# Seven-product blocks of an expert layer: when a block's last output matmuls, its input forms and the next block's attention are issued

## The chip, the cores and the metric

The kernel runs on one core of a Trainium2 chip (trn2). The metric is device time in microseconds (us), the median of three runs. The core's engines are named as the profile names them: PE (TensorE matmuls), PEld (its weight loads), DVE (VectorE), ACT (ScalarE), POOL (GpSimd) and SP (SyncE, which issues nearly all DMAs).

## The reference, cut to what matters

Attention over pooled keys and values, then two expert layers, each fed by the one before:

```python
# q, k, v: (8 batches, 8 heads, 576 rows, 64)
k_p = k.reshape(B, H, 72, 8, D).mean(axis=3)      # v_p likewise
attn = softmax(q @ k_p.T / 8) ; x = attn @ v_p    # max subtracted, sum + 1e-9
x = x as (4608, 512)                              # rows by all heads
y = (sigmoid(x @ w_gate) * (x @ w_val)) @ w_out   # d_ff = 1536
h = y @ w_in                                      # d_ff = 2048
out = where(h > 0, h, exp(min(h, 0)) - 1) @ w_out2
```

All inputs and outputs are float32. TensorE gets each float32 operand as a high and a low part, and every product is made in three passes (high·high, high·low, low·high), so that one product of a 128-row operand costs three matmuls.

## The kernel before, in words

The 4608 rows go in nine tiles of 512 rows, n = 0 to 8. Each tile n needs its attention output x (512 features, four feature tiles), then the first expert layer on it, and its y is written to DRAM. The second expert layer (from about 1190 us of the trace on) reads y back. Neither the change nor what follows touches that layer's code.

**Tiles n = 0, 1** run the first layer directly, with 512-column matmuls (the loop up to `SQ` = 2, by twelve chunks c of 128 hidden features). Beside it `plan(m)` lays out the attention of the next tile.

**Tiles n = 2 to 8 ("blocks")** use Strassen's scheme in Winograd's form for x @ w_gate and x @ w_val: x is cut into two halves of rows (`LOW`, `HIGH`, 256 columns) and two halves of features, and from these four quarters `form_x` makes seven forms (a11, a12, a22, s1 to s4), each as a high part (a rounded copy) and a low part (a subtraction). A block has twelve units, u = 0 to 11. An even unit is a chunk pair's gate, the next odd unit its value. Each unit makes seven products in the order `STEPS` (k = 0 to 6), each of six matmuls of 256 columns (line 1166, tiles `pl`). DVE and ACT put the seven products together through `u2`, `u3`, `u4` (lines 1176 to 1208), apply the sigmoid to the gate, and the value unit multiplies the two into `sg` and splits it into the high and low `g`.

**Output matmuls** ("y": line 658, 512 columns, accumulated in four `acc` banks over a whole block) follow the pair of units that made their `g`: 24 a pair, spread over the next two units' steps by `Y_FILL` through the list `fill` (`filler(n)` issues the next n of it).

**Block border.** After unit 11, `weighted` (lines 599 and 606) makes the next block's x from probabilities and values into four PSUM banks, the 24 output matmuls still in `fill` run in one go, `form_x` is written out, and the next block's units 0 and 1 have no output matmuls, since a block's first `g` comes after unit 1. The four finished `acc` banks are copied out at u = 0, k = 1, 2, 3, 6 (`FLUSH_AT`, `flush_one`) and stored.

**Attention of the next block.** `thin_plan(n+1)` hangs steps on (unit, step) positions of block n, each issued behind that step's product and output matmuls. For each of four 128-row tiles i, with u = 2 + 2i: q transposes (`q_thin`, at k = 4), scores in two halves (`s_thin`, at u, 6 and u+1, 1: line 532, with maximum and subtraction on DVE), exponential (`emit_exp`, u+1, 2), sum and normalisation (`emit_norm`, u+1, 3: lines 563 and following) and the transposed probabilities in two halves (`t_thin`, u+2, 0 and 2: line 578). All of these, and the keys' transposes, go through the one PSUM bank `at1`. Sigmoid and exponential stand in different activation tables, so ACT loads a table (`ACT_TABLE_LOAD`) at each change. Keys and values of a batch are loaded in five chunks, pooled on DVE (`pool_k` line 469, `pool_v` line 491) and placed; a block that needs a new batch has its keys loaded and pooled in its predecessor's units 0 to 4, its values in units 3 to 9. Blocks 2 to 6 prepare batches 3 to 7; block 7 has neither keys nor values to prepare.

**Background work.** `work()` takes the next piece of preparing the second layer's weights (loads, narrowing on DVE by lines 107, 111, 117 and 121, stores), 34 pieces a block at the positions `WORK_AT` and `MORE_AT`.

Each engine runs its own instructions in program order (`manual_schedule`): the positions above set the order, and an instruction that waits holds up all behind it on its engine. Output matmuls and products need no DVE step between them except through the product banks (three, `places`, two used twice and one three times a unit) and through `g`.

## Time and profile before

| | |
|---|---|
| median of three runs | 1951.09 us (1948.0 to 1951.66) |
| the profiled execution's own time | 1948.47 us |
| its span in the trace | 1946.8 us |
| PE busy in the span | 1798.2 us (92%) |
| DVE, ACT, POOL busy | 1108.1, 858.1, 635.0 us |
| from a block's `weighted` to the next one's, blocks 2 to 7 | 127.1, 121.8, 120.5, 120.2, 122.6, 112.8 us |

Read a row of the timeline as: start in the span, busy time, engine, line, operation, tile written <- tiles read, partitions x elements, count; in brackets the engine's idle time just before and what ended it. A run of matmuls of one form stands as one row, and its busy time can overlap that of the next row, so for PE the distance between starts is what counts. Rows of waits give a sum, the number of waits and the longest. Rows of windows give the busy time of each engine in a stretch, then the granted PE clock as a share of 2.4 GHz.

### The profile page before, as it was taken

The page shows a single profiled execution, that of the slowest core. Times are in us where ns is not written, and L with a number is a line of the kernel's source. Part 1 is how long each engine was busy: PE and PEld are TensorE (multiplying, and loading weights), DVE is VectorE, ACT ScalarE, POOL GpSimd, SP SyncE. Part 2 cuts the span into 40 slices and gives each one's busy share as a digit, 9 for nine tenths or more (in the row PEclk, how much of TensorE's full clock was granted, in tenths as well). Part 3 has the DMA queues.
Part 4 walks back from the last instruction along what each step waited for, and adds up shares of the span by engine and source line. Part 5 has one row for each costly group of instructions (what it writes and reads, how often), then busy time and mean ns, then how long its engine had stood idle before and what let it go on. Part 6 is the DMA issues. An engine that isn't in the chain of part 4 may idle for free.

```text
span 1946.8 us, 27943 instructions
## 1 busy us (share of the span) xinstructions
PE 1798.2 (92%) x10212; PEld 1587.7 (82%) x10212; DVE 1108.1 (57%) x2073; ACT 858.1 (44%) x1727; POOL 635.0 (33%) x635
## 2 busy tenths in 40 slices
PE   3687899799999999999999899999999999999999
PEld 2465777688887888888889788998998989989987
DVE  6799566666666667666665664533444344443432
ACT  3355344344444444434444334444454444444443
POOL 2345345334243333433333332222222222222222
PEclk8788999899999999999999999999999999999999
DMA  7254344575756757567576887334343353343431
GB/s 204 90 171 156 124 128 146 199 231 192 245 188 228 229 190 248 186 231 237 172 232 207 300 309 281 118 125 168 114 179 116 119 192 127 121 176 132 147 114 52
DMA packets 150905, 346.81 MB, mean 178 GB/s; under 512 B 47728, under 2 KB 79472, under 8 KB 150768
## 3 DMA queue, kind: packets, MB, share of 16 engines
q1 hardware_dynamic: 150768, 345.02, 51.8%
q8 instruction: 81, 1.33, 0.3%
q14 instruction: 56, 0.46, 0.1%
HBM read 287.31 MB, written 57.67 MB: 177 GB/s over the span
## 4 chain that ended last, share of the span: by engine, by line
PE 71%; DVE 18%; ACT 4%; issue 3%; DMA 3%; POOL 1%; SPq 0%; ACTq 0%; DVEq 0%; POOLq 0%
PE oacc L1327 20%; PE bank L1281 18%; PE pl L1166 15%; PE acc L658 9%; DVE nt L117 2%; PE gv L633 2%; PE ats L532 2%; DVE nt L111 1%; DMA rkv<-in_k_dram 1%; DVE nt L107 1%; DVE vs L491 1%; DVE a L95 1%; DVE ks L469 1%; PE pl L599 1%; DVE sm L563 1%
## 5 line engine op out<-in xcount | busy, mean ns | idle before, releaser
L1281 PE MATMUL bank<-form,wr 128*128 128x384 f32 x2016 | 411.0, 338 | 1.0 <-DVE u L1314 0.7
L1281 PEld LDWEIGHTS bank<-form,wr 128*128 128x128 f32 x2016 | 366.5, 188 | 29.1 <-DVE u L1314 1.1
L658 PE MATMUL acc<-g,wos 128*128 128x512 f32 x1152 | 349.5, 399 | 0.9 <-ACT g L94 0.4
L1327 PE MATMUL oacc<-w2o,gc 128*128 128x512 f32 x1080 | 288.9, 393 | 0.4 <-POOL gc L95 0.4
L1327 PEld LDWEIGHTS oacc<-w2o,gc 128*128 128x128 f32 x1080 | 199.6, 187 | 30.5 <-POOL gc L95 0.8
L658 PEld LDWEIGHTS acc<-g,wos 128*128 128x128 f32 x1152 | 192.6, 191 | 15.1 <-ACT g L94 1.2
L95 POOL TENSOR_TENSOR gc<-ea,gc 128x384 fp32r<-128x384 f32 x96 | 98.3, 1024 | 298.2 <-ACT gc L94 295.1
L95 POOL TENSOR_TENSOR g<-sg,g 128x512 fp32r<-128x512 f32 x108 | 142.6, 1330 | 161.7 <-ACT g L94 161.7
L1166 PE MATMUL pl<-s,wg 128*128 128x256 f32 x1008 | 154.7, 290 | 37.7 <-DVE u L1181 27.0
L1166 PEld LDWEIGHTS pl<-s,wg 128*128 128x128 f32 x1008 | 140.8, 192 | 57.6 <-DVE u L1181 37.3
L95 POOL TENSOR_TENSOR gc<-pair,gc 128x384 fp32r<-128x384 f32 x96 | 98.1, 1022 | 260.4 <-ACT gc L94 238.4
L1166 PE MATMUL pl<-s,tt 128*128 128x256 f32 x1008 | 154.9, 291 | 11.5 <-DVE a L95 4.4
L1166 PE MATMUL pl<-a,wg 128*128 128x256 f32 x1008 | 154.1, 289 | 5.0 <-DVE sg L1200 5.0
L1166 PEld LDWEIGHTS pl<-s,tt 128*128 128x128 f32 x1008 | 138.8, 192 | 23.4 <-DVE u L1202 4.7
L633 PE MATMUL gv<-x,wg 128*128 128x512 f32 x576 | 147.6, 411 | 10.0 <-DVE x L95 5.3
L1166 PEld LDWEIGHTS pl<-a,wg 128*128 128x128 f32 x1008 | 140.9, 192 | 18.3 <-DVE sg L1200 9.1
L1327 PE MATMUL oacc<-w2p,gc 128*128 128x512 f32 x540 | 143.2, 393 | 0.0
L633 PEld LDWEIGHTS gv<-x,wg 128*128 128x128 f32 x576 | 111.6, 198 | 36.1 <-issue 7.5
L94 ACT ACTIVATE g<-sg 128x512 fp32r<-128x512 f32 x108 | 68.1, 631 | 153.2 <-DVE sg L1203 102.7
L1327 PEld LDWEIGHTS oacc<-w2p,gc 128*128 128x128 f32 x540 | 99.8, 187 | 14.8
L1198 POOL TENSOR_TENSOR sg<-sg,u 128x256 f32<-128x256 f32 x42 | 33.6, 801 | 206.2 <-DVE u L1197 187.8
L1294 DVE SCALAR_TENSOR_TENSOR ea<-ea,bank 128x384 f32<-128x384 f32 x48 | 26.7, 555 | 117.0 <-ACT ea L1291 117.0
(199 smaller groups left out, 2861.2 us busy)
## 6 DMA issues: line engine op xcount, KB each, us to landing
wr<-wd SPq DMA_DIRECT2D x96, 896.0 KB, 6.4
tt<-td SPq DMA_DIRECT2D x84, 768.0 KB, 5.1
wos<-wd SPq DMA_DIRECT2D x96, 512.0 KB, 5.3
rw<-in_moe_w_out_dram SPq DMA_DIRECT2D x22, 512.0 KB, 3.6
r<-yd SPq DMA_DIRECT2D x24, 384.0 KB, 7.8
out_dram<-po SPq DMA_DIRECT2D x36, 256.0 KB, 2.0
rw<-in_moe_w_in_dram SPq DMA_DIRECT2D x16, 512.0 KB, 4.0
wd<-rw SPq DMA_DIRECT2D x16, 512.0 KB, 5.9
```

Source lines behind the costliest of these rows:

```text
L94: nc.scalar.activation(out=dst_hi, in_=src, func=AF.Copy)
L95: eng.tensor_tensor(out=dst_lo, in0=src, in1=f32(dst_hi), op=ALU.subtract)
L107: nc.vector.tensor_scalar(out=t.bitcast(F32), in0=t.bitcast(F32), scalar1=H_LOW, scalar2=H_HIGH, op0=ALU.max, op1=ALU.min)
L117: nc.vector.scalar_tensor_tensor(out=t, in0=r[:, :, 1], scalar=-0x40000000, in1=t, op0=ALU.bitwise_and, op1=ALU.bitwise_or)
L532: nc.tensor.matmul(a[o:o + n, i // 2, (i % 2) * w:(i % 2 + 1) * w], lhsT=qt[:, j * P + o:j * P + o + n], rhs=kbd[b % 2][:, j * w:(j + 1) * w],
L633: nc.tensor.matmul(d, lhsT=w[:, i, a_w, j], rhs=x[j][:, a_x], start=(j == 0 and a_w == 0 and a_x == 0), stop=(j == KD - 1 and a_w == 1),)
L658: return lambda: nc.tensor.matmul(acc[m], lhsT=w[:, a_w, m * P:(m + 1) * P], rhs=g[:, a_g], start=(c == 0 and a_w == 0 and a_g == 0), stop ...
L1166: nc.tensor.matmul(src, lhsT=w(a_w, j), rhs=f_t[nm][:, j, a_x], start=opens and m == 0, stop=m == 5, skip_group_check=True,)
L1198: nc.gpsimd.tensor_tensor(out=c22, in0=c22, in1=u4, op=ALU.mult)
L1281: nc.tensor.matmul(bank[b ^ flip], lhsT=wp[q][a_w][:, w, j * P:(j + 1) * P], rhs=form_tile(s, a)[j][:, a_x], start=opens and n == 0, stop= ...
L1294: nc.vector.scalar_tensor_tensor(out=e, in0=e, scalar=-1.0, in1=src, op0=ALU.add, op1=ALU.max)
L1327: return lambda: nc.tensor.matmul(acc[t + i], lhsT=g[c][:, a_g, i * P:(i + 1) * P], rhs=wo2[2 * q + e][a_w], start=opens and p == 0, stop= ...
```

## The change

Five things are moved; of the arithmetic, some rounded copies and subtractions in `form_x` go to another engine.

1. **The last output matmuls.** Of the 24 left at the border, seven run before the next block's first product; the others follow by `Y_FIRST` in units 0 and 1. The last twelve go bank by bank (`by_tile`), and `FLUSH_AT` copies the `acc` banks out at (0, 5), (0, 6), (1, 1) and (1, 4).
2. **The forms** come in three portions from a generator: a11, s3 and a12 at the border, s2, s1 and a22 behind step 0 of unit 0, s4 behind step 3. Unit 0 takes its products in the order `FIRST_STEPS`. More of the high parts are made by ACT.
3. **The attention** of a tile stands at u = 1 + 2i: q at k = 0, scores at k = 2 and 4, exponential at k = 5; sum, normalisation and transposes in the unit behind it, at k = 0, 1, 4 and 6. `emit_sum` is a step of its own, ahead of `emit_norm`.
4. **Keys** are loaded and pooled one block earlier: `thin_plan(m)` handles the values of batch m in units 2 to 9 and the keys of batch m + 1 in units 7 to 10. Batch 3's keys are handled at the end of tile n = 1 (`plan`, chunks 8 to 11).
5. **Background work** has other positions, 35 a block, none in unit 0.

The first block (n = 2) issues nine output matmuls and then all three portions at once.

```diff
+    PASSES_Y = ((0, 0), (1, 0), (0, 1))
+    def emit_sum(t, p):
+        sm = at_p.tile([P, H], F32, name="sm", tag="sm", bufs=2)
+        nc.vector.tensor_reduce(out=sm, in_=p.rearrange("p (h k) -> p h k", k=SP), op=ALU.add, axis=AX.X)
+        sums[t] = sm
...
+        if by_tile:
+            return [one(m, *x) for m in range(KD) for x in PASSES_Y]
+        return [one(m, *x) for x in PASSES_Y for m in range(KD)]
...
+            if m == SQ:
+                early[(8, 9, 9, 10, 10)[c]].append(lambda c=c: load_kv("k", b + 1, c))
+                post[(9, 9, 10, 10, 11)[c]].append(lambda c=c: pool_k(b + 1, c))
+        if m == SQ:
+            post[11].append(lambda: emit_k(b + 1))
+            early[11].append(lambda: load_q((m + 1) * TPW))
...
+            upper("a11", a11)
             for j in range(SQ):
+                nc.scalar.activation(out=rh[j], in_=d[j][:, HIGH], func=AF.Copy)
+            nc.scalar.activation(out=r3, in_=d[3], func=AF.Copy)
+            lower("a11", a11)
+            each(s3, a11, rh, ALU.subtract)
+            each(s2, dh, s3, ALU.subtract)
+            upper("s3", s3)
+            upper("a12", dl)
+            lower("a12", dl)
+            lower("s3", s3, nc.gpsimd)
+            yield
...
+            for i in range(TPW):
+                t, u = m * TPW + i, 1 + 2 * i
+                put(u, 0, q_thin, t)
+                put(u, 2, s_thin, t, 0)
+                put(u, 4, s_thin, t, 1)
+                put(u, 5, lambda t=t: emit_exp(p_new[t]))
+                put(u + 1, 0, lambda t=t: emit_sum(t, p_new[t]))
+                put(u + 1, 1, lambda t=t: emit_norm(t, p_new[t]))
+                put(u + 1, 4, t_thin, t, 0, HP)
+                put(u + 1, 6, t_thin, t, HP, NCH)
...
+            if m + 1 < B:
+                for u, k, c in ((7, 1, 0), (7, 3, 1), (8, 3, 2), (9, 1, 3), (9, 3, 4)):
+                    put(u, k, load_kv, "k", m + 1, c)
+                for u, k, c in ((8, 2, 0), (9, 0, 1), (9, 2, 2), (10, 0, 3), (10, 4, 4)):
+                    put(u, k, pool_k, m + 1, c)
...
+        Y_FIRST = ((7, 1, 1, 2, 1, 2, 0), (1, 1, 1, 0, 0, 0, 0))
+        SHAPE_AT = (0, 3)
+        FLUSH_AT = ((0, 5), (0, 6), (1, 1), (1, 4))
...
-                for k, (nm, b, opens) in enumerate(STEPS):
+                for k, (nm, b, opens) in enumerate(STEPS if u else FIRST_STEPS):
...
-                    filler(Y_FILL[i][k])
+                    filler(Y_FIRST[u][k] if u < 2 else Y_FILL[i][k])
...
-                filler(len(fill))
-                form_x(n + 1, d)
+                shapes = form_x(n + 1, d)
+                next(shapes)
+                filler(7)
```

What this does to the order of three engines follows, in the names of the program: `pl` product banks, `a` and `s` forms, `wg` and `tt` weights of the products, `acc` output banks, `wos` weights of the output matmuls, `ats` scores, `p` probabilities, `sm` their sums. PE at the border into block 4, before:

```order
L606 MATMUL pl_2690<-pt,vbd 128x256
L658 MATMUL acc<-g,wos_5077 128x512 x12
L658 MATMUL acc<-g,wos_5154 128x512 x12
L1166 MATMUL pl_2688<-a_2635,wg_338 128x256 x6
L1166 MATMUL pl_2689<-s_2636,tt 128x256 x6
L1166 MATMUL pl_2690<-s_2637,tt 128x256 x6
```

and after (a_2651 is a11, a_2655 is a12, s_2653 is s3, s_2652 is s2, s_2654 is s1):

```order
L615 MATMUL pl_2707<-pt,vbd 128x256
L667 MATMUL acc<-g,wos_5104 128x512 x7
L1206 MATMUL pl_2705<-a_2651,wg_338 128x256 x6
L667 MATMUL acc<-g,wos_5104 128x512 x5
L667 MATMUL acc<-g,wos_5190 128x512 x2
L1206 MATMUL pl_2705<-a_2655,wg_338 128x256 x6
L667 MATMUL acc<-g,wos_5190 128x512
L1206 MATMUL pl_2707<-s_2653,tt 128x256 x6
L667 MATMUL acc<-g,wos_5190 128x512
L1206 MATMUL pl_2706<-s_2652,tt 128x256 x6
```

Seventeen of the 24 have moved behind the first product, and a12 stands ahead of s3 and s2. ACT at a tile's softmax, in units 2 and 3 of block 4, before:

```order
L1188 ACTIVATE sg<-pl_2688 128x256
L953 ACTIVATE qT<-atq 128x512
L1191 ACTIVATE sg<-sg 128x256
L1194 ACTIVATE sg<-sg 128x512
L1176 ACTIVATE u_2691<-pl_2688 128x256
L558 ACT_TABLE_LOAD
L558 ACTIVATE p<-p 128x576
```

and the same tile after, in units 1 and 2:

```order
L1007 ACTIVATE qT<-atq 128x512
L696 ACTIVATE yo<-acc 128x512
L94 ACTIVATE g<-sg 128x512
L559 ACT_TABLE_LOAD
L559 ACTIVATE p<-p 128x576
L1216 ACTIVATE u_2708<-pl_2705 128x256
L94 ACTIVATE g<-sg 128x512
L573 ACTIVATE sm<-sm 128x8
```

The exponential and its table load have come to stand between the first half of `g` and the next unit's first copy of a product (line 1216). DVE in unit 1 of block 4, before:

```order
L1181 TENSOR_TENSOR u_2691<-u_2691,pl_2690 128x256
L1183 TENSOR_TENSOR u_2692<-u_2691,pl_2689 128x256
L469 TENSOR_REDUCE ks<-rkv 128x64
L111 TENSOR_SCALAR nt<-nt 128x512
L1197 TENSOR_TENSOR u_2693<-u_2692,pl_2690 128x256
L117 SCALAR_TENSOR_TENSOR nt<-rw_5101,nt 128x512
L1200 TENSOR_TENSOR sg<-sg,pl_2688 128x256
```

and after:

```order
L1221 TENSOR_TENSOR u_2708<-u_2708,pl_2707 128x256
L117 SCALAR_TENSOR_TENSOR nt<-rw_5133,nt 128x512
L1226 TENSOR_TENSOR u_2709<-u_2708,pl_2706 128x256
L545 TENSOR_REDUCE mx<-ats 128x4
L546 TENSOR_TENSOR p<-ats,mx 128x288
L1240 TENSOR_TENSOR u_2710<-u_2709,pl_2707 128x256
L121 SCALAR_TENSOR_TENSOR nt<-rw_5133,nt 128x512
L1243 TENSOR_TENSOR sg<-sg,pl_2705 128x256
```

The pooling of keys (line 469) has left this unit, and a tile's maximum and subtraction (lines 545 and 546) have come into it.

## Rows read from the trace of the kernel before

**Rows 1.** The page: busy time of each engine, share of the span, instructions.

```profile
PE 1798.2 (92%) x10212; PEld 1587.7 (82%) x10212; DVE 1108.1 (57%) x2073; ACT 858.1 (44%) x1727; POOL 635.0 (33%) x635
```

**Rows 2.** Windows, blocks 2, 4, 6, 7: length, PE, PEld, DVE, ACT, POOL, PEclk, DMA.

```profile
345.20:472.30 127.10, 116.48 (x773) 103.88 (x773) 79.30 (x170) 53.12 (x112) 44.45 (x49) 0.95 0.61 206
...
594.10:714.60 120.50, 112.17 (x780) 99.08 (x779) 80.72 (x171) 53.69 (x112) 43.35 (x46) 1.00 0.65 216
...
834.80:957.40 122.60, 113.60 (x779) 100.60 (x778) 81.66 (x170) 53.73 (x112) 42.60 (x45) 0.99 0.64 212
957.40:1070.20 112.80, 109.78 (x768) 99.69 (x767) 69.05 (x157) 51.12 (x100) 38.06 (x35) 1.00 0.63 211
```

**Rows 3.** Waits of PE from 345 to 1170 us: sum, count, longest.

```profile
PE pl L1166 <- DVE u L1181: 27.0, 30, 2.8
PE pl L1166 <- DVE u L1197: 10.5, 5, 2.6
```

**Rows 4.** Timeline of PE, border into block 4 and its units 0 to 2.

```profile
598.37 5.76 PE L658 MATMUL acc<-g,wos 128*128 128x512 f32 x24
603.96 0.88 PE L1166 MATMUL pl<-a,wg 128*128 128x256 f32 x6
...
614.55 0.88 PE L1166 MATMUL pl<-a,wg 128*128 128x256 f32 x6
615.26 0.88 PE L1166 MATMUL pl<-a,tt 128*128 128x256 f32 x6
...
617.87 0.97 PE L1166 MATMUL pl<-s,wg 128*128 128x256 f32 x6 [1.73 <-DVE u L1197]
618.81 0.97 PE L1166 MATMUL pl<-a,wg 128*128 128x256 f32 x6
...
626.51 0.60 PE L952 MATMUL atq<-ident,rq 128*128 128x128 f32 x4
626.87 0.96 PE L1166 MATMUL pl<-a,tt 128*128 128x256 f32 x6
```

**Rows 5.** Timeline, the same stretch, other engines.

```profile
599.10 0.73 ACT L94 ACTIVATE a<-xr 128x256 fp32r<-128x256 f32 x2
599.11 0.41 DVE L896 TENSOR_TENSOR xe<-xr,atv 128x256 f32<-128x256 f32 x1
...
603.01 1.45 POOL L95 TENSOR_TENSOR s<-xr,s 128x256 fp32r<-128x256 f32 x2 [1.79 <-ACT s L94]
...
616.14 1.01 DVE L469 TENSOR_REDUCE ks<-rkv 128x64 f32<-128x512 f32 x1 [1.94 <-DMA rkv<-in_k_dram]
```

**Rows 6.** Timeline, units 8 and 9 of block 2, all engines.

```profile
439.56 1.48 DVE L117 SCALAR_TENSOR_TENSOR nt<-rw,nt 128x512 int32<-128x512 int32 x1
...
441.43 0.98 PE L1166 MATMUL pl<-s,wg 128*128 128x256 f32 x6 [1.40 <-DVE u L1181]
...
443.67 1.28 ACT L1188 ACT_TABLE_LOAD   x1 [0.86 <-PE pl L1166]
444.96 0.39 ACT L1188 ACTIVATE sg<-pl 128x256 f32<-128x256 f32 x1
...
446.87 0.63 ACT L1194 ACTIVATE sg<-sg 128x512 f32<-128x512 f32 x1 [0.21 <-DVE sg L1193]
...
448.49 1.28 ACT L558 ACT_TABLE_LOAD   x1
...
451.21 0.69 ACT L558 ACTIVATE p<-p 128x576 f32<-128x576 f32 x1 [1.43 <-DVE p L545]
...
452.54 0.75 DVE L563 TENSOR_REDUCE sm<-p 128x8 f32<-128x576 f32 x1
```

**Rows 7.** Timeline of PE, first `weighted`, at the end of tile n = 1.

```profile
344.58 0.90 PE L599 MATMUL xv<-pt,vbd 128*128 128x128 f32 x3 [5.31 <-DVE sg L651]
```

**Rows 8.** Timeline of DVE, block 8.

```profile
1098.14 0.56 DVE L1090 TENSOR_TENSOR rt<-r,r 128x384 f32<-128x384 f32 x1 [4.12 <-DMA r<-yd]
```

**Rows 9.** Windows, a stretch of block 3 (columns as Rows 2).

```profile
500.00:502.50 2.50, 2.50 (x12) 2.31 (x12) 2.43 (x5) 1.50 (x3) 1.83 (x2) 0.50 1.00 364
```

More of the change, by code (lines that the diff above doesn't have):

```diff
@@ L661, in one @@
             )
-        return [one(m, 0, 0) for m in range(KD)] + [one(m, 1, 0) for m in range(KD)] + [one(m, 0, 1) for m in range(KD)]
+        if by_tile:
+            return [one(m, *x) for m in range(KD) for x in PASSES_Y]
+        return [one(m, *x) for x in PASSES_Y for m in range(KD)]
     wo_next = [0]
@@ L902, in form_x @@
-            part("s2", eh)
-            for j in range(SQ):
-                nc.vector.tensor_tensor(out=rl[j], in0=dl[j], in1=eh[j], op=sub)
-            part("s3", rh, nc.gpsimd)
-            part("a12", dl)
-            part("s1", el, nc.gpsimd)
-            part("a22", dh)
-            part("s4", rl)
+            xr = at_p.tile([P, NW], F32, name="xr", tag="p")
+            r3 = at_p.tile([P, NW], F32, name="r3", tag="qT")
+            e3, e2 = row_tile("xe3"), row_tile("xe2")
+            two = (LOW, HIGH)
@@ new lines, in each @@
+            def each(out, x, y, op):
+                for j in range(SQ):
+                    tt_(out=out[j], in0=x[j], in1=y[j], op=op)
+            a11 = [x[:, LOW] for x in d[:SQ]]
+            upper("a11", a11)
+            for j in range(SQ):
+                nc.scalar.activation(out=rh[j], in_=d[j][:, HIGH], func=AF.Copy)
[3 more added lines that the diff above has]
+            each(s2, dh, s3, ALU.subtract)
@@ L911, in fused_kernel @@
+            yield
         a2 = two_banks("atv")
@@ L913, in fused_kernel, with filler, with_next, f @@
         weighted(SQ, d)
-        last_y()
-        emit_y(SQ - 1, acc, g, C1 - 1)
-        form_x(SQ, d)
+        shapes = form_x(SQ, d)
+        fill = []
+        def filler(n):
+            for f in fill[:n]:
+                f()
+            del fill[:n]
+        def with_next(steps):
+            last = steps[-1]
+            def f():
+                last()
+                next_wo()
+            return steps[:-1] + [f]
+        for pn, pacc, pg, pc in (pend, (SQ - 1, acc, g, C1 - 1)):
+            fill += with_next(y_steps(pacc, pg, pc, wo[pn * C1 + pc], pc == C1 - 1))
+        filler(9)
+        for _ in shapes:
+            pass
         wide.close()
```

136 lines of the change are left out of this document (63 added, 73 removed), and 3 rows, old and new, of the table fresh.

## The prediction

> **What bounds the kernel now.** I read the page first: PE is busy for 1798.2 of 1946.8 us [rows 1], so an edit that leaves PE's work alone can only win what PE waits. The change touches the seven-product blocks alone, so the next view is the windows by block. Block 4 takes 120.5 us, block 7, which prepares neither keys nor values, 112.8 [rows 2]. What a block would take without waits comes from starts in PE's timeline: seven products follow each other at 0.71 us (614.55 to 615.26), the 24 output matmuls of the border take 603.96 − 598.37 = 5.59, or 0.233 each, four q transposes 0.36 (626.51 to 626.87), `weighted` 4.3 (594.10 to 598.37) [rows 2, 4]. So 84 × 0.71 + 144 × 0.233 + 4.3 + about 18 attention groups × 0.36 = 59.6 + 33.6 + 4.3 + 6.5 = 104.0 us. Block 4 waits about 16.5 us. In block 7, without the keys' transposes, it is 103.5 of 112.8. Units 0 and 1 hold a good part of it: from unit 0's first product at 603.96 to unit 2's at 618.81 is 14.85 us for 14 products of 0.71, so 4.9 is waiting. Their last wait shows why: the seventh product of unit 1 waits 1.73 us for line 1197 [rows 4], since DVE stands 1.94 us in front of a key reduction for which the load has not landed [rows 5]. The remaining 11.6 us lie in units 2 to 11.
>
> The third view is PE's waits: DVE's line 1181 (the second step of the chain that puts products together) holds PE 30 times for 27.0 us, line 1197 five times for 10.5 [rows 3]. The five are the key loads. The thirty are mostly mid-block, and an example is 441.43: PE waits 1.40 us, because DVE had begun a narrowing step of 1.48 us at 439.56 [rows 6]. So DVE's and ACT's order, not their load (80.7 and 53.7 of 120.5 us [rows 2]), decides.
>
> **The change, part by part.** The sum is made against the profiled execution, 1948.47 us, which lies 2.6 below the median.
>
> *Border and units 0, 1.* No PE instruction goes away. Before, block 4 takes 618.81 − 598.37 = 20.44 us from the end of `weighted` to unit 2 [rows 4]. After: seven output matmuls 7 × 0.233 = 1.6. The first product may overwrite its bank when the first s3 subtraction has read it: one ACT step of 256 columns from a product bank (0.39 at 444.96 [rows 6]), three DVE steps of that size (0.41 at 599.11 [rows 5]) and three hand-overs of 0.21 to 0.25 (0.21 at 446.87 [rows 6]): 2.3 to 2.4. PE waits 0.7 there. Seven products and 14 output matmuls: 5.0 + 3.3. The second portion is behind step 0, and POOL needs 1.45 for a form's two low parts [rows 5]; I allow 0.5 of waiting, between 0 and 1.5. Unit 0 ends at 11.2. Unit 1: 7 × 0.71 + 3 × 0.233 + a tile's q and scores (3 × 0.36) = 6.8. Unit 2 starts at 18.0, and 1.1 of that is attention which stood in units 2 and 3 before. Gain 20.44 − 18.0 + 1.1 = 3.5 us. The same distances taken in the other blocks that pool keys before give 3.6 to 4.3, together 19.4 for blocks 2 to 6. Block 7 has no keys before either: 0.5. ACT, which makes the high parts (0.73 for two [rows 5]) has nothing else there; the output copies that were in unit 0 now come when their bank is finished.
>
> *Block 8* has no attention beside it. Its first units gain as block 7's, about 1.6 by their starts, and DVE's wait of 4.12 us for rows of y that have just been stored [rows 8] can shrink when the block starts earlier relative to those stores, or not at all: 0 to 4, I take 1.4. Together 3.
>
> *Keys pooled a block earlier.* Five reductions of 1.01 us [rows 5] and their loads leave units 0 to 4 and come to units 8 to 10. They are the same work; the cover there is that their loads are issued one to two units (9 us each) ahead instead of two to five steps (a step is 1.2), against a wait of 1.94 [rows 5]. At nothing in the middle of the block; if a load still lands late, the wait of up to 2 us comes back in unit 8 to 10. At the end of tile n = 1 it is new: batch 3's last reduction (1.01), an ACT copy, the transposes and two copies into place stand between line 651 and the first `weighted`, for which PE already waits 5.31 us [rows 7]. Priced at 2.5, between 0 and 5.
>
> *Softmax beside the chain.* This is where a cost is added. Before, the exponential's table load runs in a pause in which ACT would wait anyway (448.49, then 1.43 of waiting, exponential at 451.21 [rows 6]). After, load and exponential stand behind the first half of `g` and ahead of the next unit's first product copy, and the sum stands on DVE ahead of line 1221 (line 1181 before). Behind the odd unit's sixth product the path is, in order: 0.71 for the product, two DVE steps of 0.42, ACT's `g` copy 0.63, table load 1.28, exponential 0.69, sum 0.75, line 1221 0.42, four hand-overs of 0.21: 6.1 us (durations from [rows 6], `g`'s copy as line 1194's 0.63). PE meanwhile has six products and some five to seven output matmuls, 5.0 to 5.6 us, until the product that needs line 1221. So PE stands 0.5 to 1.1 us, I take 1.0, once a tile. Second, q's transposes come at step 0, in the bank `at1` that the last tile's transposes filled at step 6 of the unit before; their copies queue behind the sigmoid (0.63 [rows 6]) on ACT and, on DVE, behind narrowing steps of 1.48 [rows 6]. From durations this is 0.55 us without a narrowing step in between and 2.05 with one; half, 1.3. Unit 2 also waits for its block's first `g`; I allow 1.0, between 0 and 2. So a block has 4 × (1.0 + 1.3) + 1.0 = 10.2 after against 11.6 before, by the two ends 4 to 15. The values are still pooled mid-block, so I take no gain from that difference in blocks 2 to 5, 1.5 in block 6 (122.6 against block 4's 120.5 [rows 2]), and a loss in block 7: it waits 112.8 − 103.5 = 9.3 in all [rows 2], 1.8 of them in units 0 and 1 by their starts, so 7.5 mid-block, and 10.2 is 2.7 more.
>
> *Clock.* Block 3 has a stretch at a granted clock of 0.50, 1.2 GHz [rows 9], after units 0 and 1 in which PE waited; at 0.50 six products' worth of work lose their own length again. If units 0 and 1 are dense, this goes: 1.6 taken of up to 3.5.
>
> A rule speaks against the softmax's new place. [Rows 6] show a table load of 1.28 us at 443.67 and the sigmoid at 444.96, right behind it (443.67 + 1.28 = 444.95), and another load of 1.28 at 448.49, so a switch costs 1.28 here. The Trainium skill, page "ScalarE: Activation LUTs", section "What ACT_TABLE_LOAD costs", gives about 1283 ns for the load, which agrees, plus a drain of about 1380 ns, 2.66 us a switch, of which these rows show nothing. By it the softmax path would be 1.38 longer at each of 24 tiles, an estimate of 33 us more.
>
> Sum: −19.4 − 0.5 − 3 − 1.5 + 2.7 − 1.6 + 2.5 = −20.8. 1948.47 − 20.8 = 1927.7 for a run like the profiled one; against the median 2.6 more, 1930.
>
> **Rivals.** *The border's wait just moves (same).* If the first product still waits until the whole chain of forms is done (its banks are the forms' sources), the seven fills cover only 1.6 of what the 24 covered (5.6), and units 0 and 1 gain 0.5 instead of 3.5 to 4.3 at five borders: +17, so 1945 to 1950. For it: form making took until 603.87 and more before. Against it: the first portion's path is 2.4 us.
>
> *Mid-block waits vanish too (faster).* If narrowing steps and loads in new positions no longer meet the chain, blocks 2 to 6 come near block 7's 112.8 [rows 2]: from 117 to between 111 and 113, five blocks × 4 to 6 = 20 to 30 under the forecast: 1900 to 1910; with half of it 1920. For it: 30 waits at line 1181 [rows 3] are an order's fault. Against it: narrowing steps are as many as before, and the softmax now stands in the chain.
>
> *The softmax in the chain costs more than the border gives (slower).* Place: line 1221 in even units. If each of the 24 tiles holds PE 3.6 to 4 us rather than 2.6, that is +24 to +34, and pauses of PE in every even unit can bring a clock of 0.50 as in [rows 9] (1.6 a block, some 9 in all): 1954 to 1973. It decides from 0.9 us a tile above my 2.6 (24 × 0.9 = 21). For it: 6.1 against 5.0 has no slack, and any work piece on ACT or DVE in between adds 0.6 to 1.5. Against it: only steps listed above stand there.
>
> *The page's drain.* If a switch holds ACT 1.38 us longer where it now stands in the path, 24 × 1.38 = 33 more, 1963. The trace speaks against it, so it has a chance of 0.03.
>
> **How the numbers follow.** Forecast 0.50 (1920 to 1942); mid-block waits vanish 0.22 (1900 to 1920); border unchanged 0.13, of which 0.10 falls within 0.2% of 1951 (3.9 us, about what a measurement of this kernel can tell) and 0.03 below; softmax costs more 0.12, the drain 0.03, both slower. Faster 0.50 + 0.22 + 0.03 = 0.75, same 0.10, slower 0.15. The range cuts the faster half of the second rival (0.09) and most of the slower cases (0.11), and reaches to the end of the border rival: 1910 to 1950.
>
> **What would show it.** In the profile of after: PE's first product of a block 2.3 to 2.4 us behind `weighted`, and unit 2 at about 18; no key reduction waiting in units 0 to 4, and no more than 1 us of DVE waiting for keys in units 8 to 10; waits of PE for line 1221 once a tile, about 1 us each; a table load directly ahead of each exponential, on the chain that ended last; the wait ahead of the first `weighted` 7 to 8 us; block 4 at 117, block 7 at 115. What would make it wrong: waits at line 1221 above 2 us a tile, or a block 4 below 113.

## The result and the profile after

The changed kernel takes 1979.84 us (median of four runs, 1972.76 to 1981.47) where the kernel before, beside it, takes 1951.38: a ratio of 1.0142, interval 1.0115 to 1.0170. The change is slower by 28 us; the forecast was 1930, with a range of 1910 to 1950. The profiled execution has a span of 1977.7 us against 1946.8, 30.9 more.

The page first, engines' busy time. It answers to [rows 1] and says little: PE has 4.9 us more of busy time, and 26 us more in which it does nothing.

```profile
PE 1803.1 (91%) x10212; PEld 1581.3 (80%) x10212; DVE 1111.0 (56%) x2064; ACT 856.1 (43%) x1740; POOL 641.7 (32%) x635
```

The windows of blocks 2 to 7, from one `weighted` to the next, with columns as [rows 2]:

```profile
348.26:477.45 129.19, 116.77 (x778) 101.84 (x778) 81.03 (x169) 52.69 (x115) 44.17 (x48) 0.96 0.60 190
477.45:604.25 126.80, 112.82 (x770) 98.88 (x769) 79.25 (x169) 53.20 (x113) 46.41 (x48) 0.99 0.64 207
604.25:731.52 127.27, 112.96 (x778) 98.35 (x777) 81.56 (x168) 53.11 (x113) 45.56 (x46) 0.99 0.65 208
731.52:860.45 128.93, 115.35 (x771) 101.54 (x769) 81.26 (x172) 54.57 (x114) 44.52 (x46) 0.96 0.64 208
860.45:980.52 120.07, 112.00 (x773) 98.59 (x771) 73.95 (x161) 52.02 (x106) 43.34 (x45) 0.99 0.65 210
980.52:1097.57 117.05, 109.66 (x764) 97.70 (x765) 69.94 (x156) 51.42 (x101) 37.34 (x34) 1.00 0.62 205
```

Block 4 was 120.5 and is 127.3; block 7 was 112.8 and is 117.1; only block 6 became shorter. The windows of [rows 2] begin up to 1 us away from the first `weighted` row. Counted from row to row in both traces, the first `weighted` starts 3.7 late (348.26 against 344.58), block 2 loses 1.4, blocks 3 to 5 lose 5.1, 7.0 and 9.0 us, block 6 gains 2.5, block 7 loses 4.7, and 2.6 us more are lost from block 8 on.

The border's own path does what was forecast. PE's timeline from the end of block 4's `weighted` on (answers to [rows 4]):

```profile
615.03 1.89 PE L667 MATMUL acc<-g,wos 128*128 128x512 f32 x7
617.32 0.95 PE L1206 MATMUL pl<-a,wg 128*128 128x256 f32 x6 [0.40 <-DVE xe L918]
618.11 1.77 PE L667 MATMUL acc<-g,wos 128*128 128x512 f32 x7
...
626.10 0.88 PE L1206 MATMUL pl<-a,wg 128*128 128x256 f32 x6
...
633.22 0.88 PE L1206 MATMUL pl<-a,wg 128*128 128x256 f32 x6
```

The first product starts 2.3 us behind `weighted` (forecast 2.3 to 2.4), unit 0 ends at 11.1 (11.2), unit 2 starts at 18.2 (18.0, against 20.4 before). But then PE's waits from 348 to 1202 us, in total, count and longest (answers to [rows 3], line 1221 to line 1181 there):

```profile
PE pl L1206 <- DVE u L1221: 25.6, 30, 3.3
...
PE atq L1006 <- DVE pt L95: 16.9, 18, 1.9
PE att L587 <- DVE pt L95: 11.2, 16, 1.8
...
PE pl L608 <- DVE u L1250: 4.8, 1, 4.8
```

Three more lines of the kernel before (345 to 1170 us), beside those of [rows 3]:

```profile
PE pl L1166 <- DVE sg L1200: 5.0, 11, 1.2
...
PE pl L1166 <- DVE u L1202: 3.5, 5, 0.9
...
PE att L578 <- DVE pt L95: 0.5, 2, 0.3
```

The second and third lines of after are new: 28 us in front of the copies of the transposed probabilities (`pt`), for which PE waited 0.5 us before. The total at line 1221 is no larger than at line 1181 before (25.6 against 27.0), but it stands elsewhere: 19.1 of the 25.6 are 24 waits in units 2, 4, 6 and 8 of blocks 2 to 7, one a tile. How a tile's softmax now runs shows in the timeline of block 5, units 1 to 3, all engines:

```profile
761.69 1.28 ACT L559 ACT_TABLE_LOAD   x1
...
762.99 0.69 ACT L559 ACTIVATE p<-p 128x576 f32<-128x576 f32 x1
...
763.70 0.75 DVE L565 TENSOR_REDUCE sm<-p 128x8 f32<-128x576 f32 x1 [1.90 <-ACT p L559]
...
764.37 0.41 DVE L1221 TENSOR_TENSOR u<-u,pl 128x256 f32<-128x256 f32 x1
...
764.84 0.98 PE L1206 MATMUL pl<-s,wg 128*128 128x256 f32 x6 [1.20 <-DVE u L1221]
...
767.07 1.28 ACT L1231 ACT_TABLE_LOAD   x1 [2.37 <-PE pl L1206]
...
768.37 0.38 ACT L1231 ACTIVATE sg<-pl 128x256 f32<-128x256 f32 x1
...
768.65 0.59 ACT L94 ACTIVATE pt<-att 128x512 fp32r<-128x512 f32 x1
...
769.88 0.68 DVE L117 SCALAR_TENSOR_TENSOR nt<-rw,nt 128x512 int32<-128x512 int32 x1
...
772.39 0.26 ACT L94 ACTIVATE pt<-att 128x128 fp32r<-128x128 f32 x1
...
772.69 0.29 DVE L95 TENSOR_TENSOR pt<-att,pt 128x128 fp32r<-128x128 f32 x1 [0.86 <-ACT pt L94]
...
773.03 0.66 PE L1006 MATMUL atq<-ident,rq 128*128 128x128 f32 x4 [1.48 <-DVE pt L95]
```

Read it from the top. The exponential's table load begins behind the first half of `g`; DVE waits 1.90 for the exponential, sums, and only then makes line 1221's addition, for which PE has waited 1.20. Then the sigmoid loads its own table again, 1.28 us, and the transposes' copies queue behind that sigmoid, narrowing steps and the next sigmoids; the bank `at1` is free 1.48 us after PE wants it for the next tile's q. Both table loads and both halves of the copies stand ahead of PE's two waits.

The third new loss stands at the borders of blocks 3 to 5: in blocks 4 and 5 `weighted` takes 10.8 and 10.0 us, 4.3 and 4.5 before, and in block 3 unit 2 starts 20.5 us behind `weighted`. The last steps ahead of block 4's `weighted`:

```profile
604.64 0.38 SPq L126 DMA_DIRECT2D rw<-in_moe_w_in_dram  x1
...
608.72 0.66 ACT L296 ACTIVATE nt<-rw 128x512 f32<-128x512 f32 x1 [6.12 <-DMA rw<-in_moe_w_in_dram]
...
609.48 0.43 DVE L107 TENSOR_SCALAR nt<-nt 128x512 f32<-128x512 f32 x1 [5.10 <-ACT nt L296]
609.82 0.41 DVE L1250 TENSOR_TENSOR u<-u,pl 128x256 f32<-128x256 f32 x1
...
610.29 0.78 PE L608 MATMUL pl<-pt,vbd 128*128 128x256 f32 x3 [4.81 <-DVE u L1250]
```

A piece of background work loads raw weights at 604.64, and the next piece, which narrows them, was put so close behind it that ACT stands 6.12 us in front of the load. The load itself was issued late: SP stood 7.2 us in front of it, until a store had left its buffer, so 2.0 of ACT's 6.12 us lie ahead of the issue and 4.1 behind it. ACT's wait holds DVE, DVE's holds the last addition of unit 11, and that holds PE.

### The profile page after: what moved, and what is told of

Read it like the earlier page. It is cut to its first block, busy times and chain, and to the rows that moved or that the text cites. A ratio compares the mean times of both kernels' runs of the same rounds, so it can differ in the third digit from the quotient of the medians.

```text
span 1977.7 us, 27958 instructions
## 1 busy us (share of the span) xinstructions
PE 1803.1 (91%) x10212; PEld 1581.3 (80%) x10212; DVE 1111.0 (56%) x2064; ACT 856.1 (43%) x1740; POOL 641.7 (32%) x635
## 5 line engine op out<-in xcount | busy, mean ns | idle before, releaser
L667 PE MATMUL acc<-g,wos 128*128 128x512 f32 x1152 | 362.1, 402 | 1.9 <-DMA wos<-wd 1.1
L1206 PE MATMUL pl<-s,wg 128*128 128x256 f32 x1008 | 155.9, 291 | 26.4 <-DVE u L1221 25.6
L1206 PEld LDWEIGHTS pl<-s,tt 128*128 128x128 f32 x1008 | 141.1, 192 | 14.8 <-DVE sg L1236 3.7
L1373 PEld LDWEIGHTS oacc<-w2p,gc 128*128 128x128 f32 x540 | 99.8, 187 | 14.8
L1336 ACT ACTIVATE ea<-bank 128x384 f32<-128x384 f32 x48 | 23.6, 492 | 157.5 <-PE bank L1327 157.5
```

Of the source, the lines that this page charges most:

```text
L667: return lambda: nc.tensor.matmul(acc[m], lhsT=w[:, a_w, m * P:(m + 1) * P], rhs=g[:, a_g], start=(c == 0 and a_w == 0 and a_g == 0), stop ...
L1206: nc.tensor.matmul(src, lhsT=w(a_w, j), rhs=f_t[nm][:, j, a_x], start=opens and m == 0, stop=m == 5, skip_group_check=True,)
L1336: nc.scalar.activation(out=e, in_=src, func=AF.Relu, scale=-1.0)
L1373: return lambda: nc.tensor.matmul(acc[t + i], lhsT=g[c][:, a_g, i * P:(i + 1) * P], rhs=wo2[2 * q + e][a_w], start=opens and p == 0, stop= ...
```

## The experiments

Each run is timed beside the kernel before on the same chip. "Gain" is the difference of two ratios times 1948 us, the median of before there; on that scale the changed kernel is at 1976 us. Executions of one kernel lie up to 7 us on either side of its median, and the spans of the profiled ones give the same differences within 8 us, so a gain of less than 8 us is known only roughly.

| run | median us | ratio to before | interval |
|---|---|---|---|
| changed kernel | 1979.84 | 1.0142 | 1.0115 to 1.0170 |
| e1 attention back | 1968.67 | 1.0113 | 1.0090 to 1.0136 |
| e2 work back | 1964.96 | 1.0082 | 1.0064 to 1.0100 |
| e3 fills back | 1986.34 | 1.0197 | 1.0180 to 1.0214 |
| e4 attention and work back | 1957.92 | 1.0049 | 1.0031 to 1.0068 |
| e5 border only | 1962.61 | 1.0078 | 1.0056 to 1.0101 |
| e6 = e4, keys later | 1948.02 | 0.9995 | 0.9986 to 1.0005 |
| e7 = e2, q one step on | 1941.22 | 0.9970 | 0.9957 to 0.9983 |
| e8 = e2, no table change | 1933.32 | 0.9924 | 0.9909 to 0.9939 |
| e9 = before, no table change | 1946.86 | 0.9993 | 0.9984 to 1.0002 |
| e10 = changed, q one step on | 1949.69 | 1.0002 | 0.9991 to 1.0012 |
| e11 = e7, exponential behind the copy | 1925.88 | 0.9874 | 0.9856 to 0.9892 |
| e12 = e7, ends mended | 1949.57 | 0.9999 | 0.9987 to 1.0011 |
| e13 = e11, fills back | 1930.93 | 0.9908 | 0.9891 to 0.9924 |
| e14 = e11, work as changed | 1947.49 | 0.9997 | 0.9985 to 1.0010 |

### Undoing one part at a time

**e1.** The attention's steps stand where they stood before:

```diff
-                t, u = m * TPW + i, 1 + 2 * i
-                put(u, 0, q_thin, t)
...
+                t, u = m * TPW + i, 2 + 2 * i
+                put(u + 2, 0, t_thin, t, 0, HP)
+                put(u + 2, 2, t_thin, t, HP, NCH)
+                put(u, 4, q_thin, t)
+                put(u, 6, s_thin, t, 0)
+                put(u + 1, 1, s_thin, t, 1)
+                put(u + 1, 2, lambda t=t: emit_exp(p_new[t]))
+                put(u + 1, 3, lambda t=t: emit_norm(t, p_new[t]))
```

> The changed kernel with one part undone: the next block's attention steps (q, scores, exponential, sum and normalisation, transposes, q loads) stand again at the (unit, step) positions of the kernel before; fills, forms, keys and background work stay as changed. The changed kernel's median is 1979.84 us. Theory A (the attention's order costs: transposes' copies and the next tile's q share the bank at1 with no room between them, and exponential with its table load stands in the product chain; PE waits 28 us for pt copies after, 0.5 before): 1953 to 1962, and the waits of PE for pt fall under 3 us. Theory B (background work's raw loads land late in its new positions): 1974 to 1980. Theory C (the border itself brought nothing): 1974 to 1980 too, with units 0 and 1 no shorter.

Gain 6 us (14 by the spans), where theory A asked for 18 to 27; the intervals of this run and of the changed kernel overlap. The waits for `pt` did not vanish, they moved: 9.4 us ahead of transposes and 9.1 ahead of the keys' transposes, which the change put into unit 10 and which use the same bank as the last tile's transposes there.

**e2.** Background work at its old positions:

```diff
-        WORK_AT = {(1, 0), (2, 2), (9, 4), (9, 6), (10, 1), (11, 0), (11, 2), (11, 4), (11, 5)}
...
+        WORK_AT = {(u, k) for u in range(0, C1, 2) for k in (0, 3, 4)} | {(u, k) for u in range(1, C1, 2) for k in (2, 3)}
+        WORK_AT |= {(0, 5), (1, 4), (10, 1), (11, 1)}
```

> The changed kernel with one part undone: background work stands again at the positions of the kernel before (34 pieces a block). Theory B (ACT and DVE stand 5 to 6 us in front of raw weight loads at three places, and PE waits 4.8, 2.9 and 3.2 us for it): 1964 to 1972, and DVE's wait at line 107 falls from 21 us to under 8. Theory A (only the attention's order): 1977 to 1982, since narrowing steps stand in the same chains wherever they are.

Gain 12 us, as theory B had it, and DVE's wait at line 107 is 7.9 us. The 4.8 us at block 4's border are gone. By the spans of the profiled executions it is 19, and `weighted` takes 4.3 and 4.5 us again in blocks 4 and 5. So the positions of background work were one cost, and some 12 to 16 us against the kernel before are left.

**e3.** All output matmuls ahead of the next block's first product:

```diff
-                filler(7)
+                filler(len(fill))
...
-        Y_FIRST = ((7, 1, 1, 2, 1, 2, 0), (1, 1, 1, 0, 0, 0, 0))
+        Y_FIRST = ((0,) * 7, (0,) * 7)
```

> The changed kernel with one part undone: all the output matmuls left at a block's end run ahead of the next block's first product, none in units 0 and 1; the forms' portions and all positions stay as changed. If the border gain of the prediction is real (2.5 to 3.5 us at each of seven borders): 1995 to 2003. Theory C (it brings nothing, the waits only move): 1977 to 1983.

A loss of 11 us, between the two. PE's timeline at the same border, 24 output matmuls, unit 0's first product and unit 2's first:

```profile
618.07 5.80 PE L667 MATMUL acc<-g,wos 128*128 128x512 f32 x24
623.71 0.87 PE L1206 MATMUL pl<-a,wg 128*128 128x256 f32 x6
...
637.67 0.88 PE L1206 MATMUL pl<-a,wg 128*128 128x256 f32 x6
```

19.6 us from `weighted` to unit 2, against 18.2 with the fills spread: spreading them is worth 1.4 us in block 4. In the other blocks it is 1.0 to 1.6, with 5.0 in block 3 and a loss of 1.3 in block 2; the seven borders add up to the 11. The rest of the gain at the border, 20.4 (with 1.1 of attention less) to 19.6, must lie in the forms in portions and in the keys that are no longer pooled there; no run separates the two.

**e4** undoes both, attention and work.

> Both undone, attention and background work, with the border's fills, the forms' portions and the early keys left: theories A and B together, added up, give 1938 to 1950, faster than the kernel before by part of the border's gain. If either is wrong, 1953 or more.

1958: by the ratios the parts add up (6 and 12 give the 18 found; by the spans 14 and 19 stand against 24), and it is still 10 us behind the kernel before, with the border's gain in it. A part of what remains shows in block 4's unit 10, DVE and PE:

```profile
703.36 0.28 DVE L95 TENSOR_TENSOR pt<-att,pt 128x128 fp32r<-128x128 f32 x1
703.70 1.12 PE L985 MATMUL atk<-ident,ks 128*128 128x128 f32 x4 [4.21 <-DVE pt L95]
```

The keys' transposes wait 4.21 us for the tile's transposes to leave the bank; unit 10 takes 15 to 16 us where it took 9. The other part is under e6.

### What was left: keys and row buffers

**e5** changes only the border of the kernel before; the keys' steps come one unit later.

> The kernel before with the border alone changed: output matmuls spread over units 0 and 1, forms in portions, outputs copied out late; attention, values and background work at the positions of before. Keys stay in the block in which they stood before, but one unit later (loads from unit 1, step 5 on, pooled in units 2 to 4), since the three row buffers that loads use are held by the forms and output copies until then. Theory: the border gains 3.4 us in blocks 3 to 6 and 1.5 in 7, and loses nothing later, so the kernel before less some 16 to 20 us (1928 to 1934 where before is 1948). Rival: the keys' loads set the time of units 1 to 4 and take the gain back: 1944 to 1950. Rival: mid-block waits swallow it, since what comes by DMA comes at its own pace: 1944 to 1950 with longer units 5 to 11.

Slower than before by 15 us, against the theory. Unit 2 starts 17.0 us behind block 4's `weighted` (20.4 before), so the border's gain of 3.5 is there, without attention in it. But units 3 and 4 take 12.3 and 12.9 us (8.8 and 10.0 before): in unit 3 PE waits five times, 14.4 us in all, for a copy of pooled keys. Unit 2 takes 12.9 where it took 10.9, for the reason found under e6. No run has the border's change with the keys' steps in units 0 to 2, as before: their loads use the three row buffers that the forms and output copies now hold through units 0 and 1. So the border's change, as it is written, moves the keys too; that it can't be made without that is not shown.

**e6** is e4 with the keys' steps behind the last tile's transposes:

```diff
-                put(10, 2, k_first, m + 1)
-                put(10, 6, k_last, m + 1)
+                put(10, 6, k_first, m + 1)
+                put(11, 4, k_last, m + 1)
```

> The run with attention and background work of before (1958 us), with the keys' pooling moved two to four steps on and their transposes to unit 10, step 6 and unit 11, step 4, behind the last tile's transposes. There unit 10 took 15 to 16 us instead of 9, with PE waiting 4.2 us for the bank that the tile's and the keys' transposes share. Theory (that collision is what is left of the loss): five blocks by 5 to 6 us less, 1928 to 1934, faster than the kernel before. Rival (too much DVE work at the block's end, wherever it stands): 1948 to 1958, with the waits moved to unit 11.

Gain 10.5 us, under half of the theory's 24 to 30, and no difference from the kernel before. Unit 10 still takes 12.5 to 13.3, and in blocks 4 to 6 unit 2 takes 12.8 to 13.2 where it took 10.9. Why unit 2 does shows in DVE's timeline at the end of block 4's unit 1:

```profile
616.23 0.69 DVE L694 COPY yo<-acc 128x512 f32<-128x512 f32 x1 [2.44 <-DMA yd<-yo]
```

The last output copy, at unit 1, step 4, waits 2.44 us for a row buffer whose store is still under way, and line 1243 and PE behind it (2.15). Such a wait for line 1243 stands in unit 2 of every block from 2 to 7: 14.5 us in e6, 14.5 in e5 and 14.8 in e4. In the changed kernel, e2, e7 and e11, which have the attention at its new place, no output copy waits for its row buffer. So with the attention at its old place, the late output copies take back about what the border gives.

### Bank and table

**e7** leaves the attention at its new place and moves q, scores and exponential one step on:

```diff
-                put(u, 0, q_thin, t)
-                put(u, 2, s_thin, t, 0)
-                put(u, 4, s_thin, t, 1)
-                put(u, 5, lambda t=t: emit_exp(p_new[t]))
+                put(u, 1, q_thin, t)
+                put(u, 3, s_thin, t, 0)
+                put(u, 5, s_thin, t, 1)
+                put(u, 6, lambda t=t: emit_exp(p_new[t]))
```

> The changed kernel with background work of before (1965 us), with q, both scores and the exponential one step later (k = 1, 3, 5 and 6), so that a product and two output matmuls stand between a tile's last transposes and the next tile's q in the shared bank. PE waits there 9.4 us for the transposes' copies ahead of q. Theory (the bank costs by itself): 9 us less, 1954 to 1958. Rival (the softmax in the product chain is the larger part, and the exponential one step later lengthens it): 1965 to 1980, with more wait at line 1221's counterpart (33.1 us).

Gain 22 us, more than twice the 9.4 that PE is recorded as waiting there. PE's waits of e2 (first fence) and e7:

```profile
PE pl L1205 <- DVE u L1220: 33.1, 33, 4.1
PE atq L1006 <- DVE pt L95: 9.4, 15, 1.4
```

```profile
PE pl L1205 <- DVE u L1220: 28.9, 30, 3.5
```

q's wait is gone from the list. Summed over units 2 to 10 of blocks 2 to 7, PE's recorded waits fall from 52.0 to 33.2 us: the 9.4 of q, 3.6 each at lines 1220 and 1244 and 2.3 for loads of q are the main part. What each of the four moved steps earned is not separated. In block 4 the odd units with q take 9.3, 10.0 and 9.3 instead of 10.4, 10.5 and 10.1, and unit 2 10.4 instead of 11.4. The rival falls: the exponential one step later did not lengthen line 1220's wait (28.9 against 33.1). One step of distance was worth more than the whole border.

**e8** takes the table loads away; the exponential is left out of the computation:

```diff
-                put(u, 5, lambda t=t: emit_exp(p_new[t]))
+                put(u, 5, lambda t=t: nc.scalar.activation(out=p_new[t], in_=p_new[t], func=AF.Copy, scale=SCALE))
```

> The changed kernel with background work of before (1965 us), with the blocks' exponential replaced by a plain scaled copy of the same size, so that ACT loads no table in the blocks; this part of the computation is left out, the rest stays. Two loads of 1.28 us a tile go, 24 tiles. Theory (ACT's order with exponential and loads in the chain is what the attention's new place costs): 1.28 us a tile in units 2, 4, 6, 8 at the chain's end and most of the waits for the transposes' copies: 1940 to 1948. Rival (the bank and DVE's narrowing steps, not ACT): 1958 to 1965.

Gain 31 us, more than the theory's 17 to 25. PE's waits:

```profile
PE pl L1205 <- DVE u L1220: 10.1, 10, 4.1
```

Of e2's waits at this line 23.4 us stood in units 2, 4, 6 and 8 of blocks 2 to 7, one for each of the 24 tiles; 0.4 of them are left, and q's wait for `pt` falls from 9.4 to 2.6. New are waits for loads of q (7.8 against 2.3). The 31 us are 1.28 a tile, as long as one of the two loads; that one of them was free is not shown by this.

**e9** is the control, the same edit in the kernel before:

> The kernel before with the blocks' exponential replaced by a plain scaled copy, so that no table is loaded in the blocks; this part of the computation is left out. The same edit on the changed kernel's attention (with background work of before) took 32 us off. Theory (before, exponential and loads run in ACT's pauses, and only the new place puts them on the path): 1940 to 1948 against 1948. Rival (the 48 loads cost as much wherever they stand): 1915 to 1925.

A ratio of 0.9993 (0.9984 to 1.0002): leaving out the same 48 loads there gives nothing that can be measured. It is the place, not the load.

**e11** goes the other way and keeps the loads, but puts exponential and sum where nothing in the product chain is behind them; q and scores go one more step on with them (against e7):

```diff
-                put(u, 1, q_thin, t)
-                put(u, 3, s_thin, t, 0)
-                put(u, 5, s_thin, t, 1)
-                put(u, 6, lambda t=t: emit_exp(p_new[t]))
-                put(u + 1, 0, lambda t=t: emit_sum(t, p_new[t]))
-                put(u + 1, 1, lambda t=t: emit_norm(t, p_new[t]))
-                put(u + 1, 4, t_thin, t, 0, HP)
-                put(u + 1, 6, t_thin, t, HP, NCH)
+                put(u, 2, q_thin, t)
+                put(u, 4, s_thin, t, 0)
+                put(u, 6, s_thin, t, 1)
+                put(u + 1, 0, lambda t=t: emit_exp(p_new[t]))
+                put(u + 1, 2, lambda t=t: emit_sum(t, p_new[t]))
+                put(u + 1, 3, lambda t=t: emit_norm(t, p_new[t]))
+                put(u + 1, 5, t_thin, t, 0, HP)
+                put(u + 2, 0, t_thin, t, HP, NCH)
```

> The run with background work of before and q one step later (1941 us), with the exponential moved on once more, behind the next unit's first product copy and second half of g (unit u+1, step 0), the sum to step 2 behind line 1220's addition, normalisation to step 3, transposes to step 5 and the next unit's step 0, q and scores at steps 2, 4 and 6. Then neither table load nor sum stands ahead of the addition for which PE waited 28.9 us. Theory (this chain is the rest of the softmax's cost): 1926 to 1934, that wait under 10 us. Rival (the sigmoid's own reload and DVE's narrowing steps keep the chain as long): 1938 to 1948.

Gain 19 us over e7 (15 by the medians, 11 by the spans), a ratio to before of 0.9874: the fastest version, ahead of both kernels. PE's waits in its blocks, and its windows of blocks 4 and 7:

```profile
PE att L587 <- POOL p L580: 22.0, 22, 1.6
PE pl L1205 <- DVE u L1220: 10.0, 10, 4.1
```

```profile
586.48:701.86 115.38, 109.79 (x779) 97.96 (x778) 81.97 (x170) 54.04 (x114) 46.06 (x46) 1.00 0.69 227
...
930.62:1041.38 110.76, 108.43 (x766) 98.51 (x765) 68.80 (x155) 51.54 (x102) 39.09 (x34) 1.00 0.63 212
```

The 28.9 us at the addition became 10.0, and of its waits in the tiles' even units 19.8 became 0.3; block 4 takes 115.4 with the same work on every engine, and the granted clock is 1.00 from block 3 to 7. PE now waits about 1 us a tile for POOL's normalisation, which is what a next step would move.

### What holds in which surroundings

**e10** is the changed kernel with e7's step alone.

> The changed kernel, its background work left as changed, with q, scores and exponential one step later (k = 1, 3, 5, 6). With background work of before this step took 24 us off (1965 to 1941). Theory (bank order and background work's place are two separate costs that add up: 15 us for the work): 1954 to 1960 against 1980. Rival (both are one cost, waits that shift from one to the other): 1940 to 1948, or 1965 and more.

Gain 27 us, level with the kernel before, and between the theory and the rival: the step is worth 22 with the old work positions and 27 with the new ones. The work's positions are worth 6 us here (e10 to e7; 14 by the spans).

**e13** puts the fills back on e11. (The 22.1 us in its expectation was misread from the trace; the rows under e3 say 19.6.)

> The fastest run so far (background work of before, exponential behind the product copy: 1926 us) with the border's output matmuls put back: all of them ahead of the next block's first product, none in units 0 and 1. On the changed kernel this cost only some 11 us, though units 0 and 1 with what stands ahead of them became 4.0 us longer in each of six blocks (22.1 against 18.1 in block 4). Theory (the border gain is real and the changed kernel's later waits took half of it back): here 20 to 24 us come back, 1945 to 1950. Rival (the border is worth 11 us whatever follows): 1935 to 1939.

A loss of 7 us (3 by the spans), below the rival's 9 to 13. So the spread fills are worth 1 to 1.5 us a block in either surrounding, and nothing of them was taken back by later waits: that theory falls.

**e14** puts the change's work positions on e11.

> The fastest run so far (1926 us) with background work at the positions of the change. With the bank squeezed the work's new positions cost 12 us (by ratios, 1.0142 to 1.0082), with q one step later 6 to 9. Theory (ACT stands in front of raw weight loads at the borders of three blocks, whatever the attention's order): 1933 to 1939, with ACT waiting over 15 us for raw loads of w_in. Rival (it only cost because the chains had no slack): 1924 to 1930.

A loss of 24 us (20 by the spans), more than either side expected. ACT's waits for DMA in its blocks, and those of e11 (second fence):

```profile
ACT nt L296 <- DMA rw<-in_moe_w_in_dram: 23.5, 4, 8.3
ACT nt L296 <- DMA rw<-in_moe_w_out_dram: 16.9, 5, 4.7
ACT rs L94 <- DMA wd<-rw: 12.2, 4, 6.1
```

```profile
ACT nt L296 <- DMA rw<-in_moe_w_out_dram: 22.2, 6, 7.9
ACT rs L94 <- DMA wd<-rw: 3.1, 7, 0.7
```

Four waits for raw w_in, and four of up to 6.1 us for a store to leave its buffer, are there only with the new positions. The first are those of the border above: e14's blocks 3 to 5 take 5.7, 6.9 and 7.8 us longer than e11's. The cost doesn't need chains without slack. Its size is known to within a factor only: 12, 6 and 24 us by the ratios of e2, e10 and e14, 19, 14 and 20 by the spans.

**e12** tried the two ends of the stretch, on e7:

```diff
-                early[(8, 9, 9, 10, 10)[c]].append(lambda c=c: load_kv("k", b + 1, c))
-                post[(9, 9, 10, 10, 11)[c]].append(lambda c=c: pool_k(b + 1, c))
+                early[(7, 7, 8, 8, 9)[c]].append(lambda c=c: load_kv("k", b + 1, c))
+                post[(8, 8, 9, 9, 10)[c]].append(lambda c=c: pool_k(b + 1, c))
...
+                    flush_at = ((0, 3), (0, 4), (0, 6), (1, 2)) if n == NWB - 1 else FLUSH_AT
```

> The run with background work of before and q one step later (1941 us), with the two ends mended: batch 3's keys are loaded and pooled one chunk earlier in tile n = 1 (PE waits 7.0 us there for the last key copy, 5.3 before), and in block 8 the finished outputs are copied out at steps 3, 4, 6 of unit 0 and 2 of unit 1, so that the reads of y behind them in SP's queue start earlier. Theory (first weighted 2.3 us and block 8 3.8 us late against the kernel before): 1935 to 1938. Rival (the 5.3 us at the end of tile 1 have another cause, and y's rows come at their own pace): 1939 to 1943.

Slower than e7 by 6 to 8 us. In tile n = 1 a new wait of 9.9 us for a sigmoid on ACT takes the place of the 7.0, and `weighted` starts 10.6 us later than in e7; block 8's reads of y wait 4.4 us instead of 4.3. What the row of 5.23 us in the changed kernel's block 8 comes from stays open, and so does what holds ACT in tile 1.

## Why the prediction was wrong

Between the forecast for the profiled execution (20.8 us less) and its span (30.9 more) lie 52 us. Counted from row to row in PE's timelines of before and after, they divide like this; "border" is from the end of `weighted` to unit 2, "units 2 to 10" from unit 2's start to unit 11's, and the 1.1 us of attention a block that moved from the second to the first is counted where it stood before:

| part | forecast us | measured us |
|---|---|---|
| border, blocks 2 to 7 | −19.9 | −14.6 |
| units 2 to 10, blocks 2 to 7 | +1.2 | +26.2 |
| `weighted` of blocks 4 and 5 | 0 | +12.0 |
| end of tile 1 | +2.5 | +3.7 |
| block 8 | −3 | +2.6 |
| clock | −1.6 | in the rows above |

The last 1 us lies in unit 11 and in the other `weighted`.

**Border: the path was right.** First product, unit 0, unit 1 and unit 2 came within 0.3 us of the sum in block 4, and unit 2 starts 18.2 to 18.6 us behind `weighted` in blocks 4 to 7; only block 3 took 20.5. The reason was wrong in part: of 3.3 us in block 4 the fills are 1.4 (e3), and the rest is left to the forms and the keys.

**Softmax and bank: the mechanism was right, what it was set against wrong.** Forecast were 1.0 us a tile at line 1221 and 1.3 for the bank; recorded are 0.8 (19.1 us over 24 tiles) and 1.2 (28.1, of which 11.2 are in front of the second half of a tile's own transposes, which the sum didn't have). So the new waits were sized well, even a little high. The step that failed is the next one: "a block has 10.2 after against 11.6 before", and so no loss in blocks 2 to 5. Most of the 11.6 were not waits. They are what is left of 120.5 − 104.0, a block's length less an ideal sum from starts, while [rows 2] have PE busy for 112.17 of the 120.50 us. In units 2 to 10 PE's rows have 25.4 us of recorded waits over blocks 2 to 7, 4.2 a block, and more than these the new ones did not replace. After, they have 53.1, which is 8.9 a block and near the forecast 10.2. The old ones did give way: lines 1200 and 1202 held PE for 7.2 us there and their successors hold it for 0.7, and line 1181's 16.4 became line 1221's 21.1. So 27.7 us of waiting were added where the forecast had 1.2, and the distances of starts say the same: 26.2. What is left of the distances without recorded waits hardly moved (496 us before, 494 after with the attention that left counted in); what it consists of stays open, and in e11 it is 16 us less. Some 5 of these are the background work's, below (e2). Block 7, in which no keys and values are prepared, came nearest: 4.7 longer, forecast 2.2.

**The slower rival came nearest, but not in its own way.** It named the place (line 1221 in even units), asked for 3.6 to 4 us a tile instead of 2.6, gave 1954 to 1973 and got a chance of 0.12. The time came out above even that, and a tile's recorded waits are 2.0 us, not 3.6. The place is shown: with the table loads gone (e8) or the exponential out of the chain (e11), the tiles' waits at the addition vanish, and 31 and 19 us come back. The two signs named for being wrong, more than 2 us a tile at line 1221 or a block 4 below 113, did not come either: both look at the new waits alone.

**The page's drain: not there.** From the Trainium skill, page "ScalarE: Activation LUTs", section "What ACT_TABLE_LOAD costs", an estimate of 33 us was worked out for a drain of about 1.38 us a switch. The loss was of that size, but not by that: in the rows the sigmoid starts 0.02 us behind its load (767.07 + 1.28, 768.37), so page and rows differ here, and the rows decide. What e8 gives back is recorded as PE's waits at line 1220 and for the bank.

**Background work: a term that was missing.** The new positions were listed in the change and priced at nothing. They cost 12 us on the changed kernel (e2, 19 by the spans) and 24 on e11 (e14). For the keys the prediction counted the loads and how far ahead they are issued, for `work()` it did not: a load and the step that needs it stood too close, with 4.1 us from issue to use, behind a buffer that came free late.

**The small terms.** Block 6 gained 2.5 where 1.5 and the border's 4.3 were forecast. Block 8 lost 2.6 where 3 of gain were forecast; DVE waits 5.23 for y's rows (4.12 in [rows 8]) and raw weights once more hold ACT, DVE and PE (3.22 us). Clock: block 3 has 0.99 now, as said, but block 5 fell to 0.96: after PE has waited 1.83 us, up to 845.84, for ACT's copy of pooled keys, the granted clock is 0.72 and then 0.60 of 2.4 GHz, between its two levels of 2.4 and 1.2 GHz, in two windows with columns as [rows 2]:

```profile
845.00:847.50 2.50, 1.66 (x8) 1.66 (x9) 1.72 (x5) 1.24 (x5) 2.32 (x2) 0.72 0.48 186
847.50:850.00 2.50, 2.50 (x11) 2.22 (x11) 1.39 (x2) 0.78 (x3) 0.73 (x1) 0.60 0.47 178
```

**The rival "border unchanged"** fell at once, by the rows. **"Mid-block waits vanish too"** comes nearest to e11, whose block 4 takes 115.4 where that rival had 111 to 113; it needed other positions than the change gave, and PE's waits mid-block were not gone but stood elsewhere (25.9 us in units 2 to 10 of blocks 2 to 7, 23.2 of them for POOL).

## What to carry to other kernels

A change that frees PE at one place moves the bound into the chains that run beside it, so count each chain's slack before putting anything into it: 48 table loads cost nothing measurable in one order and 31 us in another. Set new waits against old waits that the trace records, and not against a stretch's length less an ideal sum: here 11.6 us a block looked as if they could be replaced, and only 4.2 were waits. Where several steps share one bank or one ring of buffers, and where a load is followed by its user in a list of positions, the distance between the two is the price to look up: one step of distance was worth 22 us here, and the positions of background work 6 to 24.

## What the runs showed of the hardware that was not expected

Removing two table loads of 1.28 us from each of 24 tiles took 31 us off where they stand in the product chain (e8), and nothing that can be measured in the kernel before (e9). There the exponential's load (448.49 in [rows 6]) runs in a stretch in which ACT goes on to wait 1.43 us for DVE, so the load was free, although the engine does nothing else while it runs.
